# An mLSTM layer and two feed-forward layers in one scheduled kernel: the two-tile block moved to second place, the normalizer and weight splits shared differently, and a block's last output products queued tile by tile

## The chip, the cores and the metric

One NeuronCore of a Trainium2 chip runs the whole program. The metric is device time in microseconds, the median over runs. The kernel is written with explicit engines: PE (matrix products), DVE (vector), ACT (scalar), POOL (GpSimd) and SP, which here issues all DMAs.

## The reference

A recurrent attention layer (batch 4, 8 heads, 768 steps, head size 40) gives x of 3072 x 320. Two feed-forward layers (320 to 2048 to 320) follow, the first with a leaky ReLU, the second with h cos h.

```
for t in range(S):
    m_new = max(f[t] + m, i[t]); fs = exp(f[t] + m - m_new); is_ = exp(i[t] - m_new)
    C = fs * C + is_ * outer(v[t], k[t]);  n = fs * n + is_ * k[t]
    y[t] = sigmoid(o[t]) * (C @ q[t]) / max(abs(n . q[t]), 1)
x = y as (B*S, H*D)
h = x @ w_in;  x = max(0.01 * h, h) @ w_out          # layer 1
h = x @ w2_in; out = (h * cos(h)) @ w2_out           # layer 2
```

## The kernel before, in words

The 3072 tokens are 24 tiles of 128. A tile of the attention holds 64 steps of two sequences; its instructions are the `a_` functions: scores (L554), their weighting (L561), products into `po` and into the state (L575, L583, L591), the old state's share (`a_ys`), the normalizer (`a_norm`, L626 to L628), the scaled output gate (L633), the gated x (L638). `x_turn` (L469) transposes x on PE; `x_hi` (ACT) and `x_lo` (L481, L482, DVE) split it into a high and a low part, so that a product in f32 becomes three products of parts.

Tiles are grouped in blocks, `BLOCKS1` for layer 1 and `BLOCKS2` for layer 2. Per block 16 slots run, one per 128 columns of the hidden layer. In a slot PE makes the 8 "in" products (`m_in`, L705), ACT and DVE (POOL for part of layer 2) make the activation and its parts `gh` and `gl` (L753), and PE makes 3 "out" products per tile into the accumulators `acc` (`m_out`, L773). After the sixteenth slot ACT evacuates one accumulator per tile (`m_evac`) and SP stores it. The intermediate result of "in" lies in one of two PSUM banks in layer 1, and in one of four in the last block of layer 1 and in layer 2; one of the four is the bank that the transposes use too.

The weights come as 64-bit words and are decoded on the chip: L386 (DVE), L390 and L394 (ACT), L398 (POOL), L402 (DVE); `w_hi` copies the high part (ACT or DVE) and `w_lo` (L417) subtracts it. Layer 1's sixteen groups are decoded while the first tiles' attention and the first block run, layer 2's later.

What sets the order is `Schedule.run`: every piece of work is a task with a priority, engines it may run on with costs, dependencies, and buffers that it takes and frees. The planner walks through modelled time and gives each engine its next task, the first that can start, and among those that can start within `SLACK` the one with the lowest priority number. The priorities come from a table of offsets, `OFF`, and about twenty constants. The result is a fixed list per engine: on the chip an engine takes its instructions strictly in that order and waits at each for its semaphores.

Of the kernel before, what the change touches and what calls it, by code (L numbers as in the profile page):

```python
# [22 lines left out]
P = 128  # L23
# [22 lines left out]

BLOCKS1 = [4, 3, 3, 3, 3, 3, 3, 2]
BLOCKS2 = [3] * 8
LAT = 0.204
SLACK = 0.05  # L50
SLOW = 50.0
T_START = 19.114
ATT_LEAD = 11.227
BACKLOG = 0.465
HORIZON = 180.0
ATT_GAP = 17.089
ATT_STEP = 8.185
OUT_LAG = 8.751
SLOT0 = 5.678
DEC_LEAD = 5.605  # L60
BUSY = [-1.11, 44.0, 0.7, -11.9]
SPREAD = 4
TURNS = [(0, 2), (2, 4), (4, 8), (8, 12)]
GATES_AT = 40.379
TURN_LEAD = 27.165
W2 = {0: -2.233, 1: -16.869}
OFF = {
    "fb": 109.16, "kvo": 6.159, "qk": 17.437, "vext": -8.48, "scan": 108.588, "kt": 17.196, "s": 16.51, "weigh": 96.927, "out": 14.378,
    "sig": 19.521, "ys": 107.91, "norm": -34.5, "scale": 120.878, "gate": 83.183, "state": 89.383, "decay": 60.278, "tr": 76.529,
    "x2": 15.514, "l_a": -93.128, "l_g": -74.411, "l_cos": 40.715, "l_mul": 46.316, "l_gh": 57.895,  # L70
    "l_gl": 97.565, "w_round": -23.988, "w_mask": 40.019, "w_hi": -83.534, "w_lo": 94.398, "w_load": 20.018,
}
# [96 lines left out]
def mlstm_moe(ctx, tc, qk, kvo, ig, fg, w1, w2, const, out):  # L169
# [265 lines left out]
    def plan_split(l, i, p, dep):  # L435
        k = (l, i)
        sch.add(("whi", k), p, [act(WC), dve(WC, True)], w_hi, l, i, deps=[dep], take=[("w", k, 1)])
        sch.add(("w", k), p + OFF["w_lo"], [dve(WC), pool(WC)], w_lo, l, i, deps=[("whi", k)], free=[("wf", k)])
# [184 lines left out]
    def a_norm(eng, c):  # L623
        d = at[c]["d"] = ap.tile([P, H, 1], F32, tag="d", name="d")
        n = at[c]["po"].rearrange("p (h e) -> p h e", e=E1)[:, :, D:E1]
        nc.vector.tensor_scalar(d, n, -1.0, 1.0, ALU.mult, ALU.max)  # L626
        nc.vector.tensor_tensor(d, n, d, ALU.max)
        nc.vector.reciprocal(d, d)  # L628

# [11 lines left out]
    def plan_attention(n, c, j, m):  # L641
# [35 lines left out]
        sch.add(("gate", c), e - OFF["gate"], dvp(DM), a_gate, c, deps=[("scale", c)], take=[("x", k, 1)],
# [246 lines left out]
```

## Time and profile before

| | us |
|---|---|
| median of 3 runs (lowest, highest) | 839.64 (837.85, 840.19) |
| the profiled execution's own time | 839.06 |
| its span | 837.3 |
| PE busy, share of span | 816.1, 97% |
| PE weight loads | 780.0, 93% |
| DVE | 593.2, 71% |
| ACT | 421.3, 50% |
| POOL | 123.9, 15% |
| mean granted clock of PE | 0.984 |

A row of the timeline gives start and length in us, engine, source line, operation, the tile written and the tiles read, and in brackets the idle time ahead of it with what ended it. A group's row gives the count, the summed busy time and the mean length in ns of one instruction. PE's busy time includes the products L251, which compute nothing and run while PE waits at the start.

### The profile page before, as it was taken

What the parts mean: (1) busy time and instruction counts of PE and PEld (TensorE: products, weight loads), DVE (VectorE), ACT (ScalarE), POOL (GpSimd) and SP (SyncE); (2) the same over time, 40 slices, a digit from 0 to 9 for tenths busy, and PEclk for the clock granted to TensorE, in tenths of its full rate; (3) what the DMA queues carried; (4) which work ended last, traced back from release to release, by engine and by line L of the source; (5) the groups of instructions that cost most, each with busy time, mean ns of one, the idle gap of its engine ahead of it and who ended that gap; (6) DMA issues with size and microseconds to landing.
All of it is one profiled execution on the core that took longest, in us unless ns stands there. A gap on an engine that the chain in (4) does not pass through costs nothing.

```text
span 837.3 us, 19224 instructions
## 1 busy us (share of the span) xinstructions
PE 816.1 (97%) x7782; PEld 780.0 (93%) x7792; DVE 593.2 (71%) x1243; ACT 421.3 (50%) x898; POOL 123.9 (15%) x102
## 2 busy tenths in 40 slices
PE   8889999999999999999999999999989999999998
PEld 5658889999999999999999999999989999999998
DVE  7899987565655655654436987878787786868685
ACT  3366543443354443444345655556555666565654
POOL 3334320000011100010000012020110202030300
PEclk7689999999999999999999999999999999999999
DMA  9464554435344353432324400000010000000000
GB/s 234 161 211 146 159 145 130 115 126 167 121 151 131 127 166 111 151 99 78 110 96 136 136 9 17 32 17 32 17 32 16 33 14 27 17 25 17 1 25 25
DMA packets 29977, 74.56 MB, mean 89 GB/s; under 512 B 4352, under 2 KB 13696, under 8 KB 29888
## 3 DMA queue, kind: packets, MB, share of 16 engines
q1 hardware_dynamic: 29888, 73.33, 28.1%
q8 instruction: 61, 1.00, 0.5%
q14 instruction: 28, 0.23, 0.1%
HBM read 59.60 MB, written 13.71 MB: 88 GB/s over the span
## 4 chain that ended last, share of the span: by engine, by line
PE 82%; DVE 12%; ACT 3%; issue 2%; POOL 0%; DMA 0%; DVEq 0%; SPq 0%; ACTq 0%
PE acc L773 36%; PE ph L705 32%; PE pair L705 4%; DVE r L730 2%; PE po L583 2%; PE pair L554 2%; DVE r L731 2%; PE tr L469 2%; PE pair L575 2%; DVE t L727 1%; ACT r L735 1%; DVE g L741 1%; PE busy L251 1%; PE pair L591 1%; DVE wf L402 1%
## 5 line engine op out<-in xcount | busy, mean ns | idle before, releaser
L705 PE MATMUL ph<-xt,w 128*128 128x384 f32 (+2 forms) x1760 | 347.0, 341 | 3.3 <-DVE xt L482 2.5
L773 PE MATMUL acc<-w,gh 128*128 128x320 f32 x1568 | 346.9, 309 | 0.0
L705 PEld LDWEIGHTS ph<-xt,w 128*128 128x128 f32 x1760 | 299.3, 189 | 11.6 <-PE acc L773 4.3
L773 PEld LDWEIGHTS acc<-w,gh 128*128 128x128 f32 x1568 | 264.2, 188 | 2.2
L773 PE MATMUL acc<-w,gl 128*128 128x320 f32 (+1 forms) x784 | 239.0, 308 | 0.0
L713 ACT ACTIVATE gh<-ph 128x384 fp32r<-128x384 f32 (+2 forms) x124 | 61.3, 494 | 208.0 <-PE ph L705 175.9
L773 PEld LDWEIGHTS acc<-w,gl 128*128 128x128 f32 x784 | 146.1, 188 | 0.3 <-DVE gl L753 0.2
L753 DVE TENSOR_TENSOR gl<-ph,gh 128x384 fp32r<-128x384 f32 (+2 forms) x124 | 69.2, 558 | 99.6 <-ACT ph L714 99.3
L735 ACT ACTIVATE r<-r,hpi 128x384 f32<-128x384 f32 x128 | 79.1, 618 | 84.8 <-DVE r L731 84.3
L398 POOL TENSOR_TENSOR wf<-wf,raw 128x704 int32<-128x704 int32 x32 | 59.2, 1850 | 326.1 <-DVE wf L386 197.3
L753 POOL TENSOR_TENSOR gl<-g,gh 128x384 fp32r<-128x384 f32 x51 | 52.0, 1020 | 314.3 <-DVE r L731 173.4
L199 ACT CAST gh<-g 128x384 fp32r<-128x384 f32 x128 | 65.3, 510 | 37.6 <-PE acc L773 33.7
L741 DVE TENSOR_TENSOR g<-ph,r 128x384 f32<-128x384 f32 x96 | 53.3, 556 | 33.2 <-ACT r L735 31.4
L714 ACT ACTIVATE ph<-ph 128x384 f32<-128x384 f32 (+2 forms) x124 | 60.8, 491 | 0.0
L727 DVE TENSOR_SCALAR t<-t 128x384 f32<-128x384 f32 x128 | 45.9, 358 | 16.7 <-ACT t L721 16.4
L730 DVE SCALAR_TENSOR_TENSOR r<-t,ph 128x384 f32<-128x384 f32 x96 | 53.2, 554 | 3.3
L705 PE MATMUL pair<-xt,w 128*128 128x384 f32 (+1 forms) x288 | 54.6, 332 | 0.0
L721 ACT ACTIVATE t<-ph 128x384 f32<-128x384 f32 x96 | 46.0, 481 | 15.9 <-PE ph L705 13.7
L731 DVE TENSOR_SCALAR r<-r 128x384 f32<-128x384 f32 x128 | 50.5, 395 | 4.4
L705 PEld LDWEIGHTS pair<-xt,w 128*128 128x128 f32 x288 | 47.9, 188 | 0.0
L753 DVE TENSOR_TENSOR gl<-g,gh 128x384 fp32r<-128x384 f32 x77 | 42.4, 551 | 1.5 <-ACT gh L199 1.4
L199 ACT CAST xt<-tr 128x256 fp32r<-128x256 f32 x96 | 25.1, 316 | 20.7 <-PE tr L469 20.4
(97 smaller groups left out, 686.9 us busy)
## 6 DMA issues: line engine op xcount, KB each, us to landing
raw<-w SPq DMA_DIRECT2D x32, 704.0 KB, 4.4
kvo<-kvo SPq DMA_DIRECT2D x24, 484.0 KB, 4.0
raw<-qk SPq DMA_DIRECT2D x48, 192.0 KB, 3.8
w2d<-wf SPq DMA_DIRECT2D x16, 352.0 KB, 2.4
wf<-w2d SPq DMA_DIRECT2D x16, 352.0 KB, 3.4
fb<-sfd SPq DMA_DIRECT2D x40, 128.0 KB, 3.4
x2d<-o SPq DMA_DIRECT2D x24, 160.0 KB, 1.9
x<-x2d SPq DMA_DIRECT2D x24, 160.0 KB, 2.2
```

The source lines that it names most:

```text
L199: nc.scalar.copy(dst, src)
L398: nc.gpsimd.tensor_tensor(f, f, wraw.pop((l, i))[:, :, 0], ALU.add)
L705: nc.tensor.matmul(ph[:, :N], w[:, a:a + P], x[:, b, :N], start=k == 0, stop=k == 7)
L713: nc.scalar.activation(t["gh"][:, :N], h, AF.Prelu, alpha=0.01)
L714: nc.scalar.activation(h, h, AF.Prelu, alpha=0.01)
L727: nc.vector.tensor_scalar(a, a, MAGIC, -MAGIC, ALU.add, ALU.add)
L730: nc.vector.scalar_tensor_tensor(r, a, -TWO_PI, t["h"][:, :N], ALU.mult, ALU.add)
L731: nc.vector.tensor_scalar(r, r, -4.712388, 1.5707959, ALU.max, ALU.min)
L735: nc.scalar.activation(r, r, AF.Sin, bias=hpi)
L741: nc.vector.tensor_tensor(t["g"][:, :N], t["h"][:, :N], t["r"][:, :N], ALU.mult)
L753: on[eng].tensor_tensor(t["gl"][:, :N], t["g"][:, :N], t["gh"][:, :N].bitcast(F32), ALU.subtract)
L773: nc.tensor.matmul(po, a[:, s], w[:, b, e], start=i == 0 and k == 0 and j < 3, stop=i == NF - 1 and k == 2, skip_group_check=True,)
```

## The change

- The blocks of layer 1 are 4, 2, 3, 3, 3, 3, 3, 3 tiles instead of 4, 3, 3, 3, 3, 3, 3, 2.
- In the normalizer ACT takes the magnitude, and DVE then the maximum with 1 and the reciprocal, instead of three DVE instructions.
- The high parts of layer 1's weights are all copied by ACT.
- In the sixteenth slot of a block of two or three tiles, the "out" products are one task per tile, and each tile's evacuation waits for that task only.
- The constants and offsets of the planner, `SLACK` among them, and a few modelled costs have other values, so the order differs on every engine nearly from the start.

```diff
-BLOCKS1 = [4, 3, 3, 3, 3, 3, 3, 2]
+BLOCKS1 = [4, 2, 3, 3, 3, 3, 3, 3]
-SLACK = 0.05
+SLACK = 0.02
...
-ATT_LEAD = 11.227
+ATT_LEAD = 25.402
...
-DEC_LEAD = 5.605
+DEC_LEAD = 35.272
...
-        sch.add(("whi", k), p, [act(WC), dve(WC, True)], w_hi, l, i, deps=[dep], take=[("w", k, 1)])
+        sch.add(("whi", k), p, act(WC), w_hi, l, i, deps=[dep], take=[("w", k, 1)])
...
-        nc.vector.tensor_scalar(d, n, -1.0, 1.0, ALU.mult, ALU.max)
-        nc.vector.tensor_tensor(d, n, d, ALU.max)
-        nc.vector.reciprocal(d, d)
+        if eng == "ACT":
+            nc.scalar.activation(d, n, AF.Abs)
+        else:
+            nc.vector.tensor_scalar(d, d, 1.0, None, ALU.max)
+            nc.vector.reciprocal(d, d)
...
-        for j in range(m):
+        for j in range(m) if only is None else [only]:
...
+            if i == NF - 1 and m < 4:
+                for j in range(m):
+                    sch.add(("mo", k) if j == m - 1 else ("mo", k, j), p + OUT_LAG + 0.01 * j, ("PE", 3 * pe(1, DM)[1]), m_out, l, n, m, i, j,
+                            deps=[("gl", k)] + ([("mo", (l, n, i - 1))] if j == 0 else [("mo", k, j - 1)]), free=free if j == m - 1 else [])
+                continue
...
-            sch.add(("ev", l, n, j), p, act(DM, True), m_evac, l, n, j, deps=[("mo", (l, n, NF - 1))],
+            d = ("mo", (l, n, NF - 1)) if j == m - 1 or m > 3 else ("mo", (l, n, NF - 1), j)
+            sch.add(("ev", l, n, j), p, act(DM, True), m_evac, l, n, j, deps=[d],
```

The order moves most at three places. The first is DVE's queue from the weighting of the third tile's scores (L561) to the first instruction that needs that tile's products (L619). Before:

```order
L561 TENSOR_TENSOR fb<-pair,fb 128x512
L201 CAST w<-wf 128x704
L481 TENSOR_TENSOR xt<-tr,xt 128x2x128
L482 TENSOR_TENSOR xt<-tr,xt 64x128
L386 TENSOR_SCALAR wf<-raw_492 128x704
L417 TENSOR_TENSOR w<-wf,w 128x704
L330 COPY col<-acc 128x96
L619 TENSOR_TENSOR y<-pair,col 128x328
```

And now:

```order
L561 TENSOR_TENSOR fb<-pair,fb 128x512
L386 TENSOR_SCALAR wf<-raw_412 128x704
L402 SCALAR_TENSOR_TENSOR wf<-wf,sg 128x704
L330 COPY col<-acc 128x96
L481 TENSOR_TENSOR xt<-tr,xt 128x2x128
L482 TENSOR_TENSOR xt<-tr,xt 64x128
L417 TENSOR_TENSOR w<-wf,w 128x704
L386 TENSOR_SCALAR wf<-raw_471 128x704
L402 SCALAR_TENSOR_TENSOR wf<-wf,sg 128x704
L619 TENSOR_TENSOR y<-pair,col 128x328
```

One L386 and two L402 more stand between the two, and one copy of a high part (L201) fewer. The second place is further down the same queue, where the fourth tile, the last of the first block, is finished (L638, in the change L642) and split (L481). Before:

```order
L628 RECIPROCAL d<-d 128x8
L609 TENSOR_TENSOR tmp<-state_140,col 104x328
L633 TENSOR_TENSOR kvo<-kvo,d 128x320
L386 TENSOR_SCALAR wf<-raw_655 128x704
L638 TENSOR_TENSOR x<-acc,kvo 128x320
L386 TENSOR_SCALAR wf<-raw_743 128x704
L481 TENSOR_TENSOR xt<-tr,xt 128x2x128
L482 TENSOR_TENSOR xt<-tr,xt 64x128
```

And now:

```order
L631 TENSOR_SCALAR d<-d 128x8
L632 RECIPROCAL d<-d 128x8
L609 TENSOR_TENSOR tmp<-state_140,col 104x328
L637 TENSOR_TENSOR kvo<-kvo,d 128x320
L386 TENSOR_SCALAR wf<-raw_699 128x704
L642 TENSOR_TENSOR x<-acc,kvo 128x320
L481 TENSOR_TENSOR xt<-tr,xt 128x2x128
L482 TENSOR_TENSOR xt<-tr,xt 64x128
```

A decoding step no longer stands between the finished x and its split. Ahead of the last row DVE has, from the start of the program, five L402 and five L417 instead of four each, no copy of a high part instead of two, one L543 and one copy of the state more, one decay (L609) fewer, and two instructions of the normalizer per tile instead of three; L386 stands there seven times in both.

The third place is PE's queue where one block of layer 2 ends and the next begins; `ph` and `pair` are the banks of "in" (L705, now L710), `acc` those of "out" (L773, now L778), `tr` the transpose. Before, from the end of the last "out" of the old block:

```order
L773 MATMUL acc<-w,gl 128x320
L705 MATMUL ph<-xt,w 128x384 x16
L469 MATMUL tr<-ident,x_8185 128x128 x2
L469 MATMUL tr<-ident,x_8185 64x128
L705 MATMUL pair<-xt,w 128x384 x8
L773 MATMUL acc<-w,gh 128x320 x2
L773 MATMUL acc<-w,gl 128x320
```

And now, where the three tiles of the old block's last slot stand between "in" products of the new block:

```order
L710 MATMUL pair<-xt,w 128x384 x8
L778 MATMUL acc<-w,gh 128x320 x2
L778 MATMUL acc<-w,gl 128x320
L710 MATMUL ph<-xt,w 128x384 x8
L778 MATMUL acc<-w,gh 128x320 x2
L778 MATMUL acc<-w,gl 128x320
L710 MATMUL ph<-xt,w 128x384 x8
L778 MATMUL acc<-w,gh 128x320 x2
L778 MATMUL acc<-w,gl 128x320
L710 MATMUL ph<-xt,w 128x384 x8
```

Two "in" slots, a transpose and a third "in" stood together without an "out" between; now each "in" is followed by at least one tile's "out", and the transposes stand further on in the block. In layer 2 the low part `gl`, which POOL made in 51 of the 128 slots, is now made by DVE in all of them; POOL instead makes 25 of layer 1's L539 and L543, where it made 8.

## Rows read from the trace of the kernel before

**Rows 1.** The page's part 1, PE's busy time and its share of the span.

```profile
PE 816.1 (97%) x7782; PEld 780.0 (93%) x7792; DVE 593.2 (71%) x1243; ACT 421.3 (50%) x898; POOL 123.9 (15%) x102
```

**Rows 2.** The chain of waits: start and length of the first "in".

```profile
54.31 3.10 PE ph L705 x8
```

**Rows 3.** A window: length, busy us of PE, PEld, DVE, ACT, POOL, then granted clock.

```profile
50.00:60.00 10.00, 7.80 (x28) 5.37 (x29) 9.90 (x14) 3.61 (x7) 5.27 (x3) 0.83 0.67 218
```

**Rows 4.** Timeline of DVE ahead of the first block.

```profile
36.99 0.50 DVE L619 TENSOR_TENSOR y<-pair,col 128x328 f32<-128x328 f32 x1 [2.49 <-PE pair L591]
...
51.91 1.90 DVE L386 TENSOR_SCALAR wf<-raw 128x704 int32<-128x704 int32 x1
```

**Rows 5.** Timeline of POOL at the second of these places.

```profile
51.72 1.69 POOL L398 TENSOR_TENSOR wf<-wf,raw 128x704 int32<-128x704 int32 x1 [4.75 <-DVE wf L386]
```

**Rows 6.** Groups of instructions: count, busy us, mean ns, idle time before; start of the program.

```profile
L402 DVE SCALAR_TENSOR_TENSOR wf<-wf,sg 128x704 f32<-128x704 f32 x32 | 32.2, 1008 | 0.1
L417 DVE TENSOR_TENSOR w<-wf,w 128x704 fp32r<-128x704 f32 x31 | 28.6, 935 | 1.6 <-ACT w L199 1.1
L386 DVE TENSOR_SCALAR wf<-raw 128x704 int32<-128x704 int32 x32 | 17.9, 560 | 0.0
L201 DVE CAST w<-wf 128x704 fp32r<-128x704 f32 x16 | 9.3, 578 | 0.8 <-PE acc L773 0.7
L481 DVE TENSOR_TENSOR xt<-tr,xt 128x256 fp32r<-128x256 f32 x48 | 20.1, 419 | 14.4 <-ACT xt L199 14.4
L627 DVE TENSOR_TENSOR d<-po,d 128x8 f32<-128x8 f32 x20 | 3.3, 166 | 0.7
```

**Rows 7.** Timeline of PE, the two waits in the first block.

```profile
86.37 0.68 PE L575 MATMUL pair<-state,raw 40*64 40x41 f32 x32 [0.22 <-DVE fb L561]
...
95.09 0.52 PE L469 MATMUL tr<-ident,x 128*128 128x128 f32 x3 [0.93 <-DVE x L638]
```

**Rows 8.** Groups and DVE's timeline: a two-tile slot, and a tile's attention cluster.

```profile
L713 ACT ACTIVATE gh<-ph 128x256 fp32r<-128x256 f32 x12 | 4.6, 384 | 9.5 <-PE ph L705 8.6 <-PE acc L773 0.9
L753 DVE TENSOR_TENSOR gl<-ph,gh 128x256 fp32r<-128x256 f32 x12 | 5.1, 423 | 4.3 <-ACT ph L714 4.2
...
107.97 0.50 DVE L619 TENSOR_TENSOR y<-pair,col 128x328 f32<-128x328 f32 x1 [0.65 <-PE pair L591]
...
110.20 0.48 DVE L633 TENSOR_TENSOR kvo<-kvo,d 128x320 f32<-128x320 f32 x1
```

**Rows 9.** Windows over layer 2, columns as in rows 3.

```profile
460.00:500.00 40.00, 39.26 (x259) 38.71 (x258) 36.64 (x77) 24.16 (x54) 2.25 (x3) 1.00 0.24 76
500.00:600.00 100.00, 97.47 (x614) 96.08 (x613) 78.67 (x176) 59.13 (x127) 15.41 (x16) 1.00 0.08 24
600.00:700.00 100.00, 97.68 (x618) 96.84 (x617) 75.92 (x169) 58.44 (x123) 17.83 (x18) 1.00 0.07 21
700.00:800.00 100.00, 99.67 (x630) 99.11 (x629) 76.60 (x175) 60.64 (x129) 16.46 (x17) 1.00 0.06 21
```

**Rows 10.** Timeline of PE at a block boundary of layer 2 and behind it.

```profile
528.14 0.55 PE L469 MATMUL tr<-ident,x 128*128 128x128 f32 x3 [0.77 <-DVE g L741]
...
532.09 1.63 PE L705 MATMUL ph<-xt,w 128*128 128x384 f32 x8 [0.69 <-DVE xt L482]
...
534.87 1.55 PE L705 MATMUL ph<-xt,w 128*128 128x384 f32 x8
...
537.57 1.55 PE L705 MATMUL ph<-xt,w 128*128 128x384 f32 x8
```

**Rows 11.** Timeline of DVE, four slots in which it makes every gl.

```profile
537.37 0.56 DVE L741 TENSOR_TENSOR g<-ph,r 128x384 f32<-128x384 f32 x1 [0.28 <-ACT r L735]
...
545.03 0.56 DVE L741 TENSOR_TENSOR g<-pair,r 128x384 f32<-128x384 f32 x1 [0.28 <-ACT r L735]
```

**Rows 12.** Timeline of the end: ACT's evacuations and SP's stores.

```profile
832.96 1.30 ACT L199 COPY o<-acc 128x320 f32<-128x320 f32 x3 [2.71 <-PE acc L773]
...
833.41 1.30 SPq L789 DMA_DIRECT2D out<-o  x3
```

More of the change, by code (lines that the diff above doesn't have):

```diff
@@ L45 @@
 STEEP = math.atanh(0.5) / (1.06 * 2.0 ** -15)
-BLOCKS1 = [4, 3, 3, 3, 3, 3, 3, 2]
+BLOCKS1 = [4, 2, 3, 3, 3, 3, 3, 3]
 BLOCKS2 = [3] * 8
 LAT = 0.204
-SLACK = 0.05
+SLACK = 0.02
 SLOW = 50.0
-T_START = 19.114
-ATT_LEAD = 11.227
-BACKLOG = 0.465
+T_START = 16.163
+ATT_LEAD = 25.402
+BACKLOG = 0.429
 HORIZON = 180.0
[L56 to L59, printed above, removed]
-DEC_LEAD = 5.605
+ATT_GAP = 11.301
+ATT_STEP = 13.206
+OUT_LAG = 6.451
+SLOT0 = 2.559
+DEC_LEAD = 35.272
 BUSY = [-1.11, 44.0, 0.7, -11.9]
@@ L63 @@
 TURNS = [(0, 2), (2, 4), (4, 8), (8, 12)]
-GATES_AT = 40.379
-TURN_LEAD = 27.165
-W2 = {0: -2.233, 1: -16.869}
+GATES_AT = 18.859
+TURN_LEAD = 20.179
+W2 = {0: -8.486, 1: -26.828}
 OFF = {
[L68 to L71, printed above, removed]
+    "fb": 117.132, "kvo": 14.305, "qk": 13.373, "vext": 0.206, "scan": 113.123, "kt": -27.683, "s": -1.889, "weigh": 134.356, "out": 1.728,
+    "sig": 41.602, "ys": 144.171, "norm": -42.558, "scale": 136.89, "gate": 112.746, "state": 61.378, "decay": 54.572, "tr": 61.443,
+    "x2": 16.215, "l_a": -78.384, "l_g": -57.167, "l_cos": 77.728, "l_mul": 3.513, "l_gh": 58.007,
+    "l_gl": 101.205, "w_round": -66.41, "w_mask": 45.509, "w_hi": -52.232, "w_lo": 103.697, "w_load": -9.735,
 }
@@ L623, in a_norm @@
     def a_norm(eng, c):
-        d = at[c]["d"] = ap.tile([P, H, 1], F32, tag="d", name="d")
+        if eng == "ACT":
+            at[c]["d"] = ap.tile([P, H, 1], F32, tag="d", name="d")
+        d = at[c]["d"]
         n = at[c]["po"].rearrange("p (h e) -> p h e", e=E1)[:, :, D:E1]
-        nc.vector.tensor_scalar(d, n, -1.0, 1.0, ALU.mult, ALU.max)
-        nc.vector.tensor_tensor(d, n, d, ALU.max)
-        nc.vector.reciprocal(d, d)
+        if eng == "ACT":
+            nc.scalar.activation(d, n, AF.Abs)
+        else:
+            nc.vector.tensor_scalar(d, d, 1.0, None, ALU.max)
+            nc.vector.reciprocal(d, d)
     def a_scale(eng, c):
@@ L664, in plan_attention @@
             sch.add(("kt", c), e - OFF["kt"], [pool(DM), dve(DM)], a_kt, c, deps=[("kvo", c), ("scan", c)])
-        sch.add(("s", c), e - OFF["s"], ("PE", 0.62), a_scores, c, deps=[("qk", c, 0), ("qk", c, 1), ("scan", c), "clear"] + kt,
+        sch.add(("s", c), e - OFF["s"], ("PE", 0.72), a_scores, c, deps=[("qk", c, 0), ("qk", c, 1), ("scan", c), "clear"] + kt,
                 take=[("p", (c, 0), (s > 0) + (not last)), ("p", (c, 1), (s > 0) + (not last))])
@@ L668, in plan_attention @@
         sch.add(("sig", c), e - OFF["sig"], ("ACT", 0.36), a_sig, c, deps=[("kvo", c), ("exp", 2, "f"), ("exp", 2, "i")], table="sig")
-        sch.add(("out", c), e - OFF["out"], ("PE", 1.05 + (0.45 if s else 0) + (0.27 if not last else 0)), a_out, c,
+        sch.add(("out", c), e - OFF["out"], ("PE", 1.3 + (0.45 if s else 0) + (0.27 if not last else 0)), a_out, c,
                 deps=[("weigh", c), ("vext", c)] + ([("state", c - 2)] if s else []) + kt
@@ L674, in plan_attention @@
             sch.add(("ys", c), e - OFF["ys"], ("DVE", 0.82), a_ys, c, deps=[("out", c)], free=[("p", (c, 0)), ("p", (c, 1))])
-        sch.add(("norm", c), e - OFF["norm"], ("DVE", 0.55), a_norm, c, deps=[("ys", c) if s else ("out", c)], take=[("d", c, 1)])
-        sch.add(("scale", c), e - OFF["scale"], [pool(DM), dve(DM)], a_scale, c, deps=[("norm", c), ("sig", c)], free=[("d", c)])
+        sch.add(("norm", c), e - OFF["norm"], ("ACT", 0.08), a_norm, c, deps=[("ys", c) if s else ("out", c)], take=[("d", c, 1)])
+        sch.add(("rec", c), e - OFF["norm"], ("DVE", 0.3), a_norm, c, deps=[("norm", c)])
+        sch.add(("scale", c), e - OFF["scale"], [pool(DM), dve(DM)], a_scale, c, deps=[("rec", c), ("sig", c)], free=[("d", c)])
         sch.add(("gate", c), e - OFF["gate"], dvp(DM), a_gate, c, deps=[("scale", c)], take=[("x", k, 1)],
@@ L761, in m_acc, with m_out @@
         return [(a[k][:, DM:DM + DM // 2], slice(k * DM // 2, (k + 1) * DM // 2)) for k in range(2)]
-    def m_out(eng, l, n, m, i):
-        t = hid.pop((l, n, i))
+    def m_out(eng, l, n, m, i, only=None):
+        t = hid[l, n, i]
         gh, gl = t["gh"], t["gl"]
```

## The prediction

> **What bounds the kernel now.** I read the page's busy times first. PE is busy 97% of the span [rows 1], so time can be won only where PE computes nothing useful or stands still. Three views show where that is. The chain of waits gives the first "in" product at 54.31 us, 3.10 us long [rows 2]; until then PE does a little attention and many idle products, and DVE is what holds it: 9.90 of 10 us busy in the window that holds the end of that stretch [rows 3]. From there PE's timeline has two waits in the first block [rows 7], and then none that I found up to layer 2. In layer 2 the windows show idle PE time [rows 9]: 0.74 + 2.53 + 2.32 + 0.33 = 5.92 us, at block boundaries, where the timeline shows the transposes waiting for DVE's g and the next "in" for the split of x [rows 10]. Between boundaries a three-tile slot takes PE 537.57 - 534.87 = 2.70 us [rows 10]; that is PE's own pace, and the change doesn't touch it: the number of products is the same, since one two-tile block only changes its place. The end is a tail of 3 evacuations and 3 stores behind PE's last product [rows 12].
>
> So the terms are: the start, the first block, layer 1 behind it, the boundaries of layer 2, and the tail. The sum is made against the profiled execution, 839.06 us, which is 0.58 under the median of the three runs, 839.64. No change means within 0.3%, 2.5 us, about what a measurement of this kernel can tell apart.
>
> **The start.** DVE is in order and nearly always busy, so I count its work ahead of the split of the fourth tile. Added: one L402, one L417 (1.01 + 0.94, [rows 6]), one L543 (0.48, like the L633 of the same shape in [rows 8]). Removed: two high parts, now on ACT (2 x 0.58), and per tile one of the normalizer's three instructions (4 x 0.17) [rows 6]. The copy of a state that DVE gains and the decay that it loses cancel. Net +0.6 us. Against it stands DVE's longest idle time there, 2.49 us in front of L619, waiting for PE [rows 4]. In the new order one L386 and two L402 more, and one L201 fewer, stand ahead of that instruction: 0.56 + 2 x 1.01 - 0.58 = 2.0 us of the wait are filled with work that was done later before. What is left is -1.4 us. The third part can't be counted: an L386 that takes 0.56 on average took 1.90 at 51.91, while POOL ran an L398 from 51.72 to 53.41 [rows 4, 5, 6]. DVE is held by POOL there for 1.3 us. In the new order that L386 no longer stands between x and its split, but seven L386 still each set off an L398, and which DVE instruction is caught depends on 0.1 us. Bounds: two such holds fewer (-2.6) and three more (+4.0), with -1.4 giving -4.0 to +2.6. I take -1.0, a little worse than the count, because ACT's copy now stands ahead of every L417 and a late one holds DVE too.
>
> **The first block.** PE's waits of 0.22 and 0.93 us [rows 7] come from DVE being late with attention while it decodes weights. DVE now enters the block with five weight groups ready instead of four, five of its copies in the block or before it have gone to ACT, and the next block has two tiles instead of three, so one tile's attention moves out of this stretch. I take -1.0, between 0 and -1.15. The slow first "in" (3.10 us) stays: PE has too little to do ahead of it in either order.
>
> **Layer 1 behind it.** Here I found no idle time, so it can only get worse. New is a block with two-tile slots in the midst of attention. A slot lasts about two thirds of 2.70, 1.80 us, and the way from "in" to `gl` takes two ACT passes of 0.38 and DVE's 0.42 [rows 8], so DVE can be late by about 0.6 us with one slot's lead. A tile's cluster from L619 to L633 occupies it for 110.20 + 0.48 - 107.97 = 2.71 us [rows 8]. The new order lets "in" run up to three slots ahead around these clusters, so I take +0.8 for the whole of layer 1 and keep the full price for a rival. The 17 additional L539 and L543 on POOL hold DVE at times, but DVE has a wide margin there. ACT's 24 magnitudes, and its high parts, lie beside PE: ACT is half idle [rows 1].
>
> **The boundaries of layer 2.** The old order puts two "in" slots, a transpose and a third "in" in a row, so PE asks for PSUM banks faster than DVE returns them. The new order puts one tile's three "out" products, a third of 9, behind each of three "in" products, lets ACT empty an accumulator while PE does the next "in", and moves the transposes away from the boundary. The waits of [rows 10] should go. Late next: the transposes still share a bank with "in" and each still waits for some g, and the next "in" of that bank for the split. I take three quarters of 5.92, -4.4 us; bounds 0 and -5.9. The cover for this term is DVE: it now makes all 128 `gl`, which POOL made in 51 slots. Rows show it doing so: from 537.37 to 545.03 it made three slots' work with every `gl` in 7.66 us, 2.55 a slot [rows 11], under PE's 2.70. Three splits a block are still to be added, each an L481 of 0.42 [rows 6] and a smaller L482, some 0.7 us: 16 x 2.55 + 2.1 = 42.9 against PE's 16 x 2.70 and three transposes of 0.5 [rows 7], 44.7. It fits, narrowly.
>
> **The tail.** ACT's three copies take 1.30 us from PE's last product [rows 12]. The first two need only their own tile's products now, and can run under the 6 products behind them, so 2 x 0.43 = 0.87 us go, as long as stores follow at once: SP's issues are 0.43 apart too. I take -0.85; bounds -0.4 and -0.9.
>
> **Sum:** -1.0 - 1.0 + 0.8 - 4.4 - 0.85 = -6.45, so 832.6 beside the profiled 839.06, and with the 0.58 that the median lies above it, **833.2 us**.
>
> **Rivals.**
>
> *The stalls of layer 2 only move.* Each of the three transposes of a block still waits for a bank and for DVE, which is fuller than before. For it: DVE's margin of 1.8 us a block. Against it: the two boundaries of 2 us are gone in any case, and the slots between have several slots' lead. The term becomes 0: 837.6 us. Chance 0.17.
>
> *DVE is held by POOL more often in the start.* The magnitude now goes to a small tile in SBUF, and the maximum with 1 (L631) reads it there instead of PSUM, four times ahead of the first block. Three more holds of 1.3 us put the start at +3.0 instead of -1.0: 837.2. Chance 0.13. The Trainium skill speaks for it ("SBUF — State Buffer", Who interferes with whom): a VectorE `tensor_scalar` between SBUF tiles may use the port pair that GpSimd uses, and whoever comes second blocks for the whole instruction; by that, the trace's 1.90 us L386 agrees, and L631 would be one more instruction that can be caught.
>
> *The two-tile block starves PE.* If its "in" slots get no lead, each of three tiles' clusters costs 2.71 - 0.6 = 2.1 us: 833.2 - 0.8 + 6.3 = 838.7. Chance 0.08.
>
> *DVE becomes the bound of layer 2, and the kernel slower.* In [rows 11] every g waits 0.28 us for ACT's cosine. One more such wait in each slot makes 2.83: 16 x 2.83 + 2.1 = 47.4 against 44.7, 2.7 us a block, 22 over eight, and no gain at the boundaries: 833.2 + 4.4 + 22 = 860. It decides from (44.7 - 2.1) / 16 = 2.66 us a slot on; the rows say 2.55, and a margin of 0.11 is small. Against it: without POOL beside it DVE isn't held, and if DVE falls behind, the cosine is ready when it comes to g. Chance 0.06.
>
> *The tile-by-tile outputs do nothing* because ACT reaches the evacuations too late anyway: only the tail and part of the boundary term go, a case inside the forecast's range.
>
> **The numbers.** The forecast has 0.56: 833.2, faster. Of the first two rivals half lies beyond 2.5 us, half within. Faster 0.70, same 0.20, slower 0.10 (DVE as the bound, and some of the two-tile block with a bad start). The range takes the best ends of start, block, boundaries and tail (839.64 - 4.0 - 1.15 - 5.9 - 0.9 = 827.7) as its lower end, and reaches up past the three middle rivals to 840.5, leaving out mainly the DVE rival.
>
> **What would show it.** Right: the first "in" at 52 to 54 us; PE without waits from there to layer 2; under 2 us of idle PE between the boundaries of layer 2 in windows like [rows 9], with DVE some 85% busy and POOL at nothing; the last copy of ACT 0.43 us behind PE's last product. Wrong: a first "in" behind 56 us with DVE instructions of over 1.5 us beside L398; waits of "in" for `gl` in the two-tile block; slots of layer 2 longer than 2.70 us with PE waiting for DVE in each.

## The result and the profile after

The changed kernel takes 830.22 us (median; 829.47 to 831.19) beside 839.28 (837.85 to 840.19) for the kernel before, a ratio of 0.9894, interval 0.9875 to 0.9913: faster, by 9.1 us. 833.2 was predicted. The profiled execution took 830.75 us with a span of 829.0; before it was 839.06 and 837.3.

Part 1 of the page of the changed kernel answers to [rows 1]:

```profile
PE 813.4 (98%) x7782; PEld 781.0 (94%) x7792; DVE 602.0 (73%) x1250; ACT 430.8 (52%) x925; POOL 85.4 (10%) x68
```

PE's timeline of the kernel before, at the second "in" of the first block, the first "in" of layer 2, and the last "out":

```profile
57.91 2.11 PE L705 MATMUL ph<-xt,w 128*128 128x512 f32 x8
...
470.34 1.56 PE L705 MATMUL ph<-xt,w 128*128 128x384 f32 x8
...
833.49 0.31 PE L773 MATMUL acc<-w,gl 128*128 128x320 f32 x1
```

The same three of the changed kernel:

```profile
58.17 2.11 PE L710 MATMUL ph<-xt,w 128*128 128x512 f32 x8
...
468.65 1.55 PE L710 MATMUL ph<-xt,w 128*128 128x384 f32 x8
...
825.20 0.30 PE L778 MATMUL acc<-w,gl 128*128 128x320 f32 x1
```

These starts cut the program into segments without a modelled end in them. The start, up to the second "in", is 0.26 us longer (58.17 - 57.91). From there to layer 2 it is 410.48 us instead of 412.43, so -1.95. Layer 2, from its first "in" to the last "out", is 356.55 instead of 363.15, so -6.60. The sum, -8.29, is the difference of the spans; behind the last "out" nothing changed. The medians lie 9.06 us apart, 0.77 more than this pair of profiles.

The cut in front of layer 2 doesn't part the same work in both kernels. "Out" products of layer 1's last two slots still stand behind layer 2's first "in": 12 where the last block of layer 1 has two tiles, 18 where it has three (1164 and 1170 "out" products follow that "in" in all). Three of them take 0.44 us from start to start, so the six take 0.88. On equal work the way to layer 2 is 1.07 us shorter, and layer 2 is 7.48 us shorter. **Nine tenths of the gain lie in layer 2.**

The windows of the changed kernel answer to [rows 9]:

```profile
460.00:500.00 40.00, 38.92 (x244) 38.48 (x243) 35.24 (x78) 23.42 (x49) 0.00 (x0) 1.00 0.16 53
500.00:600.00 100.00, 100.00 (x640) 99.90 (x639) 85.09 (x194) 60.96 (x129) 0.00 (x0) 1.00 0.08 24
600.00:700.00 100.00, 100.00 (x636) 99.91 (x635) 86.06 (x194) 62.07 (x130) 0.00 (x0) 1.00 0.07 22
700.00:800.00 100.00, 100.00 (x637) 99.91 (x636) 86.60 (x198) 61.77 (x130) 0.00 (x0) 1.00 0.06 21
```

PE is idle for 1.08 us instead of 5.92, DVE is 85 to 87% busy and POOL does nothing. The one wait that is left is a single row of the waits of PE from 130 to 825 us:

```profile
PE pair L710 <- DVE g L746: 1.1, 1, 1.1
```

### The profile page after: what moved, and what is told of

It reads as the page before. It is cut to its first block, busy times and chain, and to the rows that moved or that the text cites. A ratio compares the mean times of both kernels' runs of the same rounds, so it can differ in the third digit from the quotient of the medians.

```text
span 829.0 us, 19156 instructions
## 1 busy us (share of the span) xinstructions
PE 813.4 (98%) x7782; PEld 781.0 (94%) x7792; DVE 602.0 (73%) x1250; ACT 430.8 (52%) x925; POOL 85.4 (10%) x68
## 4 chain that ended last, share of the span: by engine, by line
PE 91%; DVE 3%; ACT 0%; issue 0%
PE acc L778 41%; PE ph L710 36%; PE pair L710 6%; PE po L583 2%; PE tr L469 2%; PE pair L554 2%; PE pair L575 1%; DVE w L417 1%; PE pair L591 1%; DVE wf L402 0%; ACT w L199 0%; PE busy L251 0%; DVE r L735 0%; DVE g L746 0%; DVE y L619 0%
## 5 line engine op out<-in xcount | busy, mean ns | idle before, releaser
L778 PE MATMUL acc<-w,gh 128*128 128x320 f32 x1568 | 348.0, 309 | 0.0
L710 PE MATMUL ph<-xt,w 128*128 128x384 f32 (+2 forms) x1760 | 344.1, 338 | 0.1
L710 PEld LDWEIGHTS ph<-xt,w 128*128 128x128 f32 x1760 | 297.2, 188 | 5.7 <-PE busy L251 0.6
L778 PEld LDWEIGHTS acc<-w,gh 128*128 128x128 f32 x1568 | 264.2, 188 | 2.5
L778 PE MATMUL acc<-w,gl 128*128 128x320 f32 (+1 forms) x784 | 238.7, 308 | 0.0
L778 PEld LDWEIGHTS acc<-w,gl 128*128 128x128 f32 x784 | 145.9, 188 | 0.3 <-DVE gl L758 0.2
L398 POOL TENSOR_TENSOR wf<-wf,raw 128x704 int32<-128x704 int32 x32 | 60.7, 1897 | 270.8 <-DVE wf L386 143.1
L758 DVE TENSOR_TENSOR gl<-g,gh 128x384 fp32r<-128x384 f32 x128 | 70.5, 550 | 5.5 <-ACT gh L199 5.5
L710 PE MATMUL pair<-xt,w 128*128 128x384 f32 x288 | 56.1, 337 | 1.1 <-DVE g L746 1.1
L710 PEld LDWEIGHTS pair<-xt,w 128*128 128x128 f32 x288 | 49.4, 188 | 1.4 <-DVE g L746 1.4
L736 DVE TENSOR_SCALAR r<-r 128x384 f32<-128x384 f32 x128 | 46.1, 360 | 4.4
L417 DVE TENSOR_TENSOR w<-wf,w 128x704 fp32r<-128x704 f32 x32 | 32.5, 1016 | 1.7 <-ACT w L199 1.1
```

Of the source, the lines that this page charges most:

```text
L398: nc.gpsimd.tensor_tensor(f, f, wraw.pop((l, i))[:, :, 0], ALU.add)
L710: nc.tensor.matmul(ph[:, :N], w[:, a:a + P], x[:, b, :N], start=k == 0, stop=k == 7)
L736: nc.vector.tensor_scalar(r, r, -4.712388, 1.5707959, ALU.max, ALU.min)
L758: on[eng].tensor_tensor(t["gl"][:, :N], t["g"][:, :N], t["gh"][:, :N].bitcast(F32), ALU.subtract)
L778: nc.tensor.matmul(po, a[:, s], w[:, b, e], start=i == 0 and k == 0 and j < 3, stop=i == NF - 1 and k == 2, skip_group_check=True,)
```

## The experiments

Each run is compared with the kernel before, measured with it on the same chip. The segments are read from PE's timeline as above: the start of the second "in", the time from there to layer 2, and layer 2.

| kernel | median us | ratio (interval) | second "in" at | to layer 2 | layer 2 |
|---|---|---|---|---|---|
| before | 839.28 | | 57.91 | 412.43 | 363.15 |
| changed | 830.22 | 0.9894 (0.9875, 0.9913) | 58.17 | 410.48 | 356.55 |
| before, gl on DVE | 841.95 | 1.0035 (1.0025, 1.0046) | 56.81 | 412.41 | 366.12 |
| before, outs by tile | 835.60 | 0.9956 (0.9944, 0.9969) | 57.97 | 412.84 | 359.82 |
| before, both of these | 834.60 | 0.9947 (0.9935, 0.9959) | 55.28 | 414.49 | 358.08 |
| changed, whole outs | 867.04 | 1.0329 (1.0304, 1.0353) | 59.05 | 414.12 | 390.33 |
| changed, gl on POOL | 831.85 | 0.9910 (0.9895, 0.9925) | 59.05 | 410.48 | 357.34 |
| changed, normalizer on DVE | 829.16 | 0.9888 (0.9870, 0.9906) | 55.64 | 410.55 | 356.61 |
| changed, five high parts on DVE | 833.83 | 0.9937 (0.9924, 0.9951) | 58.84 | 411.48 | 356.71 |
| changed, one step later | 830.78 | 0.9901 (0.9886, 0.9916) | 57.66 | 411.26 | 356.55 |
| changed, three steps later | 830.70 | 0.9896 (0.9882, 0.9909) | 54.93 | 413.25 | 356.56 |
| changed, idle products doubled | 834.28 | 0.9948 (0.9935, 0.9961) | 60.13 | 410.14 | 356.56 |
| changed, blocks of before | 838.88 | 0.9998 (0.9990, 1.0007) | 62.80 | 413.50 | 357.98 |
| before, blocks of the change | 847.30 | 1.0094 (1.0079, 1.0108) | 55.75 | 414.14 | 371.99 |

In the last two columns 18 "out" products of layer 1 are counted with layer 2 where a three-tile block ends layer 1 (the changed kernels but for "blocks of before", and "blocks of the change"), and 12 in the others. To compare the two kinds, add 0.88 us to "to layer 2" of the former and take it from their "layer 2".

Layer 2 repeats to 0.2 us where its order is the same (356.55 to 356.71 in six of the rows). The second "in" doesn't: the three kernels with the start of the kernel before lie at 56.81, 57.97 and 55.28 (57.91 in that kernel itself), two with the start of the changed kernel both at 59.05 (58.17). One profile can't price an edit to the start; the medians can.

### Layer 2: order, POOL, or the outs

**1. The kernel before with every gl of layer 2 on DVE.** PE's list stays the same to the last row.

```diff
-                sch.add(("gl", k), p + OFF["l_gl"], [dve(N), pool(N)], m_lo, ...
+                sch.add(("gl", k), p + OFF["l_gl"], dve(N), m_lo, ...
```

> Edit: the kernel before, with every gl of layer 2 on DVE (51 of 128 were on POOL); PE's list of instructions stays the same to the last row. Theory 'order' (the stalls of layer 2 come from the order in which PE asks for banks and split tiles): PE's idle time from 460 to 800 us stays between 4 and 6.5 us (5.92 in the kernel before), time 837 to 841, no difference that can be measured. Rival 'POOL' (the stalls come from POOL's gl, 1.02 us each, or from POOL holding DVE): idle falls under 2 us and the time to 832 to 835. Third: DVE, with 51 x 0.56 us more, becomes late everywhere: over 842.

PE's waits from 460 to 825 us, us in total, times, longest. Kernel before:

```profile
PE ph L705 <- DVE xt L482: 2.5, 7, 0.7
PE tr L469 <- DVE g L741: 2.2, 2, 1.5
...
```

With gl on DVE:

```profile
PE ph L705 <- DVE xt L482: 5.3, 7, 0.9
PE tr L469 <- DVE g L741: 1.8, 6, 0.5
...
```

Layer 2 grew by 2.97 us, and PE was idle for 8.1 us from 460 to 800 instead of 5.92, more than "order" had expected. The waits are for the same two things, and that for the split of x doubled: PE's order still asks for it at each boundary, and DVE, with more to do, gives it later. POOL is not the cause of the stalls; taking it out of that order even costs.

**2. The kernel before with the tile-by-tile outs alone.** The change's lines on these three places are taken over, nothing else.

```diff
-        for j in range(m):
+        for j in range(m) if only is None else [only]:
...
+            if i == NF - 1 and m < 4:
...
-m_evac, l, n, j, deps=[("mo", (l, n, NF - 1))],
+m_evac, l, n, j, deps=[("mo", (l, n, NF - 1)) if j == m - 1 or m > 3 else ("mo", (l, n, NF - 1), j)],
```

> Edit: the kernel before, with only the tile-by-tile outs of the sixteenth slot added; constants, blocks, normalizer and weight copies as before. The planner then puts one tile's out behind each of three ins at the block boundaries; POOL keeps about 50 gl of layer 2. Theory 'order': the waits at the boundaries themselves go, those at the two ins that stand side by side further on may stay: idle of PE from 460 to 800 us 1 to 3 us, time 834 to 837. Rival 'tile-by-tile does nothing': 838.5 to 840. If the whole gain of layer 2 is this edit's, idle is about 1 us and the time about 833.

Layer 2 gains 3.33 us, a good two fifths of the change's 7.48 on equal work, with 2.6 us of idle PE from 460 to 800. Its waits from 460 to 825 us:

```profile
PE ph L705 <- DVE g L741: 0.9, 1, 0.9
PE ph L705 <- DVE xt L482: 0.7, 2, 0.4
PE tr L469 <- PE pair L705: 0.5, 1, 0.5
```

The wait for xt at seven boundaries is down to two places, as "order" has it, though POOL still makes about 50 gl.

**3. The kernel before with both edits**, the diffs of 1 and 2 together.

> Edit: the kernel before with both the tile-by-tile outs and every gl of layer 2 on DVE; constants as before. Segments by PE's records, from the first in of layer 2 to the last out: kernel before 363.15 us, gl on DVE alone 366.12, outs alone 359.82, the changed kernel 356.55. Theory 'order': two ins still stand side by side once in each block, so a wait of 0.3 to 0.6 us per block stays, and without POOL the rest goes: 357.5 to 360, time 833.5 to 836. Rival 'the two edits add up': 362.8, 838.5. Rival 'the two edits are all that layer 2 needs': 356.5, 832.5.

358.08: the two don't add up (that would be 362.8). The same edit that cost 2.97 us in the old order gains 1.74 in the new one. On equal work the changed kernel is another 2.4 us shorter in layer 2. That is left to the rest of the change; the planner's constants are the likely part, and no run tests them alone.

**4. The changed kernel with 48 gl on POOL**, each other instruction in its place.

```diff
+        if l == 1 and i % 5 in (1, 3):
+            eng = "POOL"
         on[eng].tensor_tensor(t["gl"][:, :N], t["g"][:, :N], t["gh"][:, :N].bitcast(F32), ALU.subtract)
```

> Edit: the changed kernel with 48 of the 128 gl of layer 2 on POOL again (slots 1, 3, 6, 8, 11, 13 of each block), the order of every other instruction untouched. Theory 'order': PE stays without waits in layer 2 but for the one of about 1 us at its start, time 830 to 831.5. Rival 'POOL': a gl on POOL takes 1.02 instead of 0.55 us, outs or ins wait, idle PE from 460 to 800 over 3 us, time 833 to 837.

The group of the last instruction ahead of the cosine, first in the changed kernel and then in this run:

```profile
L736 DVE TENSOR_SCALAR r<-r 128x384 f32<-128x384 f32 x128 | 46.1, 360 | 4.4
```

```profile
L736 DVE TENSOR_SCALAR r<-r 128x384 f32<-128x384 f32 x128 | 62.9, 492 | 4.4
```

POOL does hold DVE (0.49 instead of 0.36 us on the mean), and layer 2 loses only 0.79 us by it. The new order has room for that.

**5. The changed kernel with the outs of the sixteenth slot as one task.**

```diff
-            if i == NF - 1 and m < 4:
+            if False:
...
-            d = ("mo", (l, n, NF - 1)) if j == m - 1 or m > 3 else ("mo", (l, n, NF - 1), j)
+            d = ("mo", (l, n, NF - 1))
```

> Edit: the changed kernel with the outs of the sixteenth slot as one task again; everything else of the change stays, planner included. PE's order in layer 2 then has one place per block with in, transpose, in side by side, at the boundary. Theory 'order': each boundary stalls again by 0.3 to 0.6 us, 2 to 4 us of idle PE from 460 to 800 (1.08 in the changed kernel), time 831.5 to 834. Rival 'tile-by-tile is the whole cause': idle 5 to 6 and 835 to 837. Rival 'other constants are the whole cause': 830 to 831.

Not 2 to 4 us but 34 in layer 2, and no theory had it. The timeline of one boundary, all engines:

```profile
627.55 0.49 PE L469 MATMUL tr<-ident,x 128*128 128x128 f32 x3
...
629.14 0.99 POOL L758 TENSOR_TENSOR gl<-g,gh 128x384 fp32r<-128x384 f32 x1 [46.53 <-ACT gh L199]
629.26 1.09 DVE L736 TENSOR_SCALAR r<-r 128x384 f32<-128x384 f32 x1
630.27 0.41 DVE L481 TENSOR_TENSOR xt<-tr,xt 128x256 fp32r<-128x256 f32 x1
...
631.12 2.90 PE L710 MATMUL ph<-xt,w 128*128 128x384 f32 x8 [3.08 <-DVE xt L482]
633.82 0.73 PE L778 MATMUL acc<-w,gh 128*128 128x320 f32 x2
```

The last tile of the next block is transposed only at the boundary, between two ins; its split stands on DVE behind L736, and the block's one gl on POOL holds that L736 for 1.09 us instead of 0.36. PE waits 3.08 us, and then its products are slow: eight take 2.90 instead of 1.55. The windows show why (the granted clock stands behind POOL's busy time):

```profile
628.00:631.00 3.00, 0.04 (x1) 0.00 (x0) 2.84 (x6) 1.62 (x6) 0.99 (x1) 0.85 0.27 81
631.00:637.00 6.00, 5.88 (x20) 5.91 (x21) 2.72 (x6) 1.99 (x5) 0.00 (x0) 0.51 0.09 30
637.00:640.00 3.00, 3.00 (x21) 3.00 (x20) 1.49 (x5) 0.90 (x2) 0.00 (x0) 1.00 0.00 0
```

Behind the wait the clock is at its lower level, 1.2 instead of 2.4 GHz, until 637 us, so this wait is paid about twice. PE has seven such waits in layer 2 (in total, times, longest):

```profile
PE ph L710 <- DVE xt L482: 22.5, 7, 3.8
```

Behind five of them the clock fell. Behind the two that ended at 583.60 and 730.48 us, 3.14 us each, it stayed at 1.00, so the length of the wait doesn't decide it alone (another of 3.14 us, at 681.36, was followed by the lower clock). The window behind the first of the two:

```profile
584.00:590.00 6.00, 6.00 (x40) 6.00 (x39) 3.95 (x10) 2.70 (x6) 0.00 (x0) 1.00 0.07 27
```

Blocks took 47.6 us from first "in" to first "in" with the wait alone and 49.1 to 50.9 with the lower clock behind it, instead of 44.2. The waits account for some 21 of the 34 us, and the lower clock for most of the rest. That an idle TensorE falls back to half its clock is what the Trainium skill says ("TensorE: Matmul & The Clock Gate", Part 1: The HAM clock gate), and the trace agrees at five of the seven waits. The waits of the kernel before, 1.5 us at most, left the clock at 1.00 [rows 9].

### The start and the first block

**6. The changed kernel with the magnitude back on DVE**, order untouched.

```diff
-            nc.scalar.activation(d, n, AF.Abs)
+            nc.vector.tensor_scalar(d, n, -1.0, 1.0, ALU.mult, ALU.max)
+            nc.vector.tensor_tensor(d, n, d, ALU.max)
         else:
-            nc.vector.tensor_scalar(d, d, 1.0, None, ALU.max)
             nc.vector.reciprocal(d, d)
```

> Edit: the changed kernel with the magnitude of the normalizer back on DVE (three small DVE instructions again, no ACT), the order of everything else untouched. Theory: worth little. DVE gets 0.17 us more per tile, four times ahead of the first in, and loses the way over ACT: start within 0.7 us of the changed kernel's, time 829.5 to 831. Rival 'the magnitude on ACT bought part of the gain': 831.5 or more. Rival 'the way over ACT and the hold of L631 cost the start its gain': 829 or less.

829.16 us, with an interval that overlaps that of the change: no gain of this part can be measured. It is the fastest median of all, but not one that can be told from the changed kernel's. Three of its four executions had a mean granted clock of 0.988 to 0.990 and took 829.73 us at most; the fourth had 0.979 and took 832.15.

**7. The changed kernel with five high parts on DVE**, order untouched.

```diff
     def w_hi(eng, l, i):
+        if l == 0 and i in (0, 1, 4, 7, 9):
+            eng = "DVE"
```

> Edit: the changed kernel with the five high parts (groups 0, 1, 4, 7, 9) that DVE copied in the kernel before on DVE again, order untouched. Theory: each costs DVE about 0.58 us; two or three lie ahead of the first split, so the second in comes 0.5 to 1.5 us later, and the two behind it fall into the first block, where DVE is full, and bring back part of its waits (0.3 to 1 us): time 830.8 to 832.5. Rival 'the copies on ACT are a link too many' (the L417 of the changed kernel waited 0.4 us for ACT): 829 to 830.2.

In the profile the second "in" came 0.67 us later and the way to layer 2 took 1.00 longer, with two waits of PE for gl in the first block, 0.7 us together; the median rose by 3.6. The copies on ACT are worth 1.7 us by the profiles (0.67 of it within the spread of the start), more by the medians, and are the largest single part that could be undone with nothing else moved.

**8. and 9. Decoding steps put off**, by moving entries in the finished list: in 8 the L417 of group 4 behind the fourth tile's split, in 9 also the L386 and L398 of group 6, and the L417 of group 3 into the gap ahead of that split.

```diff
+        behind((w_round, 0, 6), (x_lo, 0, 0, 3))
+        behind((w_bits, 0, 6), (x_lo, 0, 0, 3))
+        behind((w_lo, 0, 4), (x_lo, 0, 0, 3))
+        behind((w_lo, 0, 3), (a_gate, 3))
```

> Edit: the changed kernel, with one DVE instruction moved: the subtraction L417 of weight group 4, which stood ahead of the fourth tile's L619, now behind that tile's split. Theory 'the start was lost to decoding that stands ahead of L619 and is held by POOL' (L417 at 48.40 us took 2.18 instead of 0.88, and L619 came at 50.50 though its products were done at 48.73): the first in starts about 1.8 us earlier, 53.4 to 54.4 us by the profile, PE gets no new waits of note in the first block, since the groups are three slots ahead there, and the time is 828.0 to 829.3. Rival 'DVE is simply full up to 70 us': what is put off is paid by PE in the first block, 829.7 to 831.

> Edit: the changed kernel, with three decoding steps put off: L417 of group 3 from ahead of the fourth tile's L561 to the gap between its L642 and its split (where DVE waited 1.26 us), L417 of group 4 and L386 of group 6 (with the L398 that it sets off) behind the split. Theory as for the run with one step: L561 1.2 us earlier, L619 3 us earlier, the split 3 to 3.6 us earlier, first in at 51.8 to 53, time 826.3 to 828 if the first block has no new waits. Rival 'DVE is full up to 70 us': PE waits 2 to 3 us more in the first block, time 829.5 to 831.

Neither gained. In 9 the second "in" came at 54.93, 3.24 us earlier, and the way to layer 2 took 413.25 instead of 410.48, 2.77 longer. PE's waits of that run from 54 to 126 us:

```profile
PE acc L778 <- ACT gh L718: 1.1, 1, 1.1
PE acc L778 <- DVE gl L758: 1.0, 1, 1.0
PE tr L469 <- DVE x L642: 0.3, 1, 0.3
```

The rival holds: the work that DVE is spared ahead of the split it still owes in the first block, and the wait moves there. An earlier "in" is not lost as such, though. Where DVE's list is the same, layer 2 starts earlier or later by as much as the fourth tile's split (L482) ends earlier or later: run 1 against the kernel before, 1.13 and 1.12 us earlier; run 4 against the changed kernel, 0.88 later both times; run 6 against it, 2.51 and 2.46 earlier, with one small instruction more per tile. Run 3 has the order of run 2 up to layer 2; its second "in" came 2.69 us earlier than that of run 2 but the split only 1.08, and at layer 2 1.04 were left. So what counts up to the end of the first block is how far DVE is in its work: less of it (run 7) or less waiting helps, another order of the same work does not.

**10. The changed kernel with the idle products doubled.** PE's clock is low in the start; windows of the kernel before, of the change and of this run, in that order:

```profile
20.00:40.00 20.00, 16.76 (x364) 13.46 (x368) 16.05 (x41) 6.62 (x13) 6.73 (x5) 0.67 0.51 176
```

```profile
20.00:40.00 20.00, 18.70 (x300) 14.49 (x302) 16.95 (x41) 8.43 (x18) 8.79 (x6) 0.50 0.54 175
```

```profile
20.00:40.00 20.00, 16.86 (x352) 10.60 (x351) 19.75 (x44) 9.81 (x20) 8.58 (x6) 0.96 0.51 166
```

```diff
-        nc.tensor.matmul(gt["busy"], gt["idle"], ...
+        for _ in range(2):
+            nc.tensor.matmul(gt["busy"], gt["idle"], ...
```

> Edit: the changed kernel with each of the 64 idle products L251 of the start issued twice, order untouched; they compute nothing. Theory 'the start is lost to PE's low clock': in the changed kernel the granted clock was 0.50 from 18.4 to 42.3 us and DVE waited 2.8 us for PE products there, in a run where it was 1.00 from 22 to 32 us it waited 0.8 and the second in came 2.5 us earlier. If more idle products bring the clock up there, the second in comes 1 to 3 us earlier and the time is 827.5 to 829.5. Rival 'they stand in PE's way': at the low clock each costs some 0.4 us more, the second in comes 1 to 4 us later, time 831 to 834. If they do neither: 829.5 to 831.

The clock came up to 0.96 there, and the second "in" came 1.96 us later all the same. DVE's largest wait from 10 to 58 us:

```profile
DVE fb L534 <- PE acc L522: 2.9, 2, 2.1
...
```

In the changed kernel that wait (L533 there) was 1.7 us. All the same the fourth tile's split ended only 0.23 us later (56.08 instead of 55.85). The rest of the 1.96 us lies in PE's own list, where nine idle products (2.12 us) stand ahead of the first "in" and six (1.48) ahead of the second; in the changed kernel it is five (1.25) and three (0.82). The idle products stand in PE's way, and so cost more than the clock brings. Clock and time go together from execution to execution: of the 47 executions of the kernel before that were taken beside these runs, the 10 with a mean granted clock of 0.980 or less took 840.1 us at the median, the 17 with 0.986 or more 838.5. What the low clock alone costs stays open: in the profiled execution of run 6 it was 0.78 on the mean from 20 to 40 us, and the second "in" came at 55.64, but no run sets the clock and leaves the rest alone.

### The two-tile block and the constants

**11. and 12.** `BLOCKS1` of the kernel before in the changed kernel, and that of the change in the kernel before, the planner run with each.

```diff
-BLOCKS1 = [4, 2, 3, 3, 3, 3, 3, 3]
+BLOCKS1 = [4, 3, 3, 3, 3, 3, 3, 2]
```

> Edit: the changed kernel with BLOCKS1 as before (two-tile block last), the planner run with it. Theory: the place of the two-tile block is worth about 1 us, through the first block, whose waits come back when a three-tile block follows it (0.5 to 1.2 us), the rest of layer 1 being PE's own pace in either order; from the second in to the first in of layer 2 410.5 to 412 us (410.48 in the changed kernel, 412.43 in the kernel before), layer 2 unchanged at 356.5, time 830 to 832.5. Rival 'worth nothing': 410.5 and 830. Rival 'the two-tile block in second place costs': under 410 and under 829.5.

> Edit: the kernel before with the two-tile block in second place, nothing else; the planner run with its old constants. It completes a square: old constants and old blocks 839, new constants and new blocks 830, new constants and old blocks 838.9. Theory 'blocks and constants belong together' (a planner's constants fit one sequence of blocks): no gain from the blocks alone, 838 to 844, with the waits of layer 2 as in the kernel before (363 us from its first in to the last out) and from the first in to layer 2 no less than 416.6. Rival 'the place of the block is a gain of its own': 414 to 415.5 there, and 835.5 to 837.5.

Old and old 839, new and new 830, the crossed pairs 838.9 and 847.3, more than the 844 that the theory allowed. In 12 layer 2 took 371.99 us, beside 364.03 in the kernel before on equal work, with waits from 465 to 842 us of

```profile
PE ph L705 <- DVE xt L482: 5.3, 7, 3.8
PE tr L469 <- DVE g L741: 5.0, 2, 3.6
```

though the edit is in layer 1: the planner set another order there too. In 11 layer 2 (357.98) is 2.3 us longer than the changed kernel's on equal work, and most of the loss lies ahead of it; "out" products stand ahead of the second "in" there, so from the first "in", at 54.92 us, it took 421.38 to layer 2, beside 416.60 in the kernel before and, on equal work, 414.28 in the changed one. These runs give the block's place no price of its own. A run that changes one part and plans anew prices the part and its fit with the rest together; runs 1 to 3, 5, 11 and 12 are of that kind (in run 1 PE's list stayed the same), runs 4 and 6 to 10 are not.

## Why the prediction was right or wrong

**Layer 2: right, and too small.** -4.4 was predicted with -5.9 as its end, and it is -7.48 on equal work (-6.60 between the cuts). The cause was named rightly (runs 1 to 4: the order at the boundary, with POOL secondary), and the waits went. Undersized was the total that was taken as available: the idle time of [rows 9], 5.92 us, isn't all that was lost. In PE's timeline of the kernel before, at one boundary:

```profile
576.23 0.31 PE L773 MATMUL acc<-w,gl 128*128 128x320 f32 x1
576.71 0.58 PE L705 MATMUL ph<-xt,w 128*128 128x384 f32 x2 [0.17 <-DVE xt L482]
```

From start to start 0.48 us passed, where 0.15 is usual between an "out" and what follows it; the row gives 0.17 as idle, because the modelled end of the product covers the rest. Such a wait cost 0.33. Blocks took 44.6 us from first "in" to first "in" at most boundaries of the kernel before, and take 44.2 now. The rival by which the stalls only move fell. So did that of DVE as the bound: a slot stayed at 2.70 us (the changed kernel's ins start at 598.67 and 601.37), and DVE is at 85 to 87%.

**The start: wrong.** -1.0 was taken; the second "in" came 0.26 us later in the profiled pair. By the medians the start may have gained up to some 0.5, if all that they differ by beyond the profiles lies there; the spread between executions is larger than either. The step that failed is "2.0 us of the wait are filled with work that was done later before", taken as 2.0 us less of idle DVE. They were filled: L619 waited 0.29 us at 33.80 where it had waited 2.49 [rows 4]. But other waits took their place. Windows up to the end of the fourth tile's split, of the kernel before and of the changed one:

```profile
0.00:54.45 54.45, 43.90 (x753) 30.33 (x764) 46.21 (x97) 21.32 (x37) 18.21 (x20) 0.77 0.63 185
```

```profile
0.00:55.85 55.85, 45.20 (x753) 31.39 (x764) 45.75 (x94) 24.09 (x44) 21.31 (x20) 0.76 0.66 193
```

DVE's busy time fell by 0.46 us, where +0.6 was counted, and its idle time grew from 8.24 to 10.10 us, where -2.0 was counted. On DVE's timeline of the changed kernel:

```profile
18.02 1.22 DVE L533 TENSOR_TENSOR_SCAN fb<-acc,eye 128x512 f32<-128x512 f32 x1 [1.11 <-PE acc L521]
...
23.20 0.50 DVE L201 COPY state<-pair 104x328 f32<-104x328 f32 x1 [0.83 <-PE pair L591]
23.61 0.60 DVE L631 TENSOR_SCALAR d<-d 128x8 f32<-128x8 f32 x1
...
42.24 0.89 DVE L402 SCALAR_TENSOR_TENSOR wf<-wf,sg 128x704 f32<-128x704 f32 x1 [0.96 <-POOL wf L398]
...
43.98 2.18 DVE L417 TENSOR_TENSOR w<-wf,w 128x704 fp32r<-128x704 f32 x1
...
48.40 2.18 DVE L417 TENSOR_TENSOR w<-wf,w 128x704 fp32r<-128x704 f32 x1 [0.41 <-ACT w L199]
...
55.11 0.43 DVE L481 TENSOR_TENSOR xt<-tr,xt 128x256 fp32r<-128x256 f32 x1 [1.26 <-ACT xt L199]
```

PE, at its low clock (run 10's windows), and POOL were late instead. The longest of these waits is the last: the L386 that no longer stands between x and its split had run in the time in which PE and ACT turn x, and DVE now idles there for 1.26 us. Two L417 were held by POOL, 2.18 us instead of 0.94 on the mean [rows 6]; the kernel before had two holds too, the L386 of [rows 4] and one of the two L417 that took 2.55 us together from 45.97, so this term hardly changed. The chain gives the first "in" like this, answering to [rows 2]:

```profile
55.60 1.85 PE ph L710 x8
```

It starts 1.29 us later, and is 1.25 shorter, since the clock was up by then (1.00 from 53 to 58 us, 0.66 in the kernel before); the prediction had it that it "stays" slow. At 55.60 us it lies between the signs named for it, 52 to 54 for right and behind 56 for wrong. So the second "in" came only 0.26 later. The rival on L631 was seen once: 0.60 us beside an L398 from 22.50 to 24.19, where it takes 0.16 alone, so the rule that the prediction named from the Trainium skill ("SBUF — State Buffer", Who interferes with whom) holds for it. Run 6 shows that this cost the kernel nothing that can be measured. What bounds start and first block together is DVE's work and its waits (runs 1, 4, 6 and 9), and an argument on the first "in" alone was one on the wrong quantity.

**The first block: right.** -1.0 predicted; PE's two waits of [rows 7], 1.15 us, became one of 0.28:

```profile
96.35 0.52 PE L469 MATMUL tr<-ident,x 128*128 128x128 f32 x3 [0.28 <-DVE x L642]
```

Run 7 shows the copies on ACT as a cause.

**Layer 1 behind it: +0.8 predicted, and no loss.** PE was busy for 330.00 of 330.00 us from 130 to 460 in both kernels, so the two-tile block starved nothing. Of the -1.07 us to layer 2 on equal work the waits of the first block are 0.87; the other 0.2 stay unassigned.

**The tail: wrong.** -0.85 predicted, nothing came. The changed kernel's last rows answer to [rows 12]:

```profile
824.67 1.30 ACT L199 COPY o<-acc 128x320 f32<-128x320 f32 x3 [2.71 <-PE acc L778]
...
825.12 1.30 SPq L794 DMA_DIRECT2D out<-o  x3
```

The copies start 0.53 us ahead of PE's last product, at 825.20. They did so before: 832.96 against 833.49. "ACT's three copies take 1.30 us from PE's last product" misread [rows 12], whose start was never set beside that of the last product. The first copy waits for its own accumulator's last product in both kernels; the planner's task stands for three tiles, the semaphore for one. So the tile-by-tile outs can act through the order alone here. The sign that was named for the tail, ACT's last copy 0.43 us behind PE's last product, was seen (0.47) but tells nothing: in the kernel before it was 0.46.

That the sum came out close, -8.29 against -6.45, is in part luck: start and tail gave 2.1 us less than predicted, the first block 0.1 less, and layer 2 (3.1) and layer 1 behind the first block (1.0) gave more.

## What to carry to other kernels

Measure a stall from the start of one product to the start of the next; idle time by modelled ends showed 4.84 of 7.48 us here. Where a segment is cut at an instruction, count what stands on either side in both orders: 0.88 us lay on different sides here. Before undoing a part of a planned order, freeze the order, or the run prices the planner's new order (34 us for undoing an edit that gains 3.33 by itself). Where an engine such as DVE bounds a whole stretch, putting its work off gains little (3.24 us earlier, 2.77 paid back); taking work off it, or waits away from it, does.

## What the runs showed of the hardware that was not expected

- Waits of 3.08 to 3.76 us were followed by a PE clock of 0.50 five times out of seven, once for about 6 us (run 5); two waits of 3.14 us left it at 1.00, and so did the waits of layer 2 in the kernel before, 1.5 us at most.
- PE's records can be nearly full (18.70 of 20.00 us, run 10's second window) at a granted clock of 0.50; with twice the idle products the clock was 0.96 at 16.86 us busy.
- The same list of instructions reached the second "in" at 55.28 to 57.97 us, while layer 2 repeated to 0.2 us where its order was the same: in these profiles the spread between executions arises in the start. Executions with a lower mean granted clock took longer (run 10); whether the clock is the cause isn't shown.
